# A Trainium2 kernel's start-up rebuilt: two plain first steps, a first chunk in halves, later operand sums, halo rows from DRAM

## The chip, the cores and the metric

The kernel runs on one core of one Trainium2 chip. The metric is the device time of one execution in microseconds; the time before is 1448.68 us, the median of three runs (1447.93 to 1449.42).

## The reference

Two layers follow each other. The first is a causal convolution of seven taps along the sequence, with softmax weights per head of 24 channels. The second turns each value into a phase pair, mixes the tokens with two 4224 x 4224 matrices and ends with a channel mix.

```python
# x: (8, 4224, 192), weight: (8, 7); w = softmax(weight) over the taps
x_pad = concat([zeros((B, 6, D)), x], axis=1)
x = einsum('hk,bskhg->bshg', w, unfold(x_pad, 7))      # the convolution

theta = x @ w_theta                                    # (192, 192)
zr, zi = x * cos(theta), x * sin(theta)
yr = einsum('ts,bsd->btd', w_tok_r, zr)                # (4224, 4224)
yi = einsum('ts,bsd->btd', w_tok_i, zi)
u = x + yr + yi
out = u + maximum(u @ w_ch, 0)
```

All inputs and the output are float32; the kernel computes in float16 with float32 sums.

## The kernel before

**Tiles.** The 4224 tokens are cut into 33 chunks of 128 on the input side (`NK`) and 33 blocks of 128 on the output side (`NT`). A chunk is not 128 neighbouring tokens: it takes 32 (`Q`) from each quarter of the sequence (`token`). All 8 batches and 192 channels lie side by side, 1536 columns, and these are split into two halves of each batch's channels, 768 columns each (`HN`).

**A chunk's life** (class `Chunk`, line 177). `__init__` loads x into `xw`, casting to float16, with four DMAs from Pool (line 197), one for each quarter, and gives every 32 tokens 16 rows of history in front (`HALO`), so `xw` has 2 x 48 rows. The history of most chunks is copied from the chunk before, inside the chip's memory, by four DMAs on SP (line 188); chunks 0, 11 and 22 read it from DRAM with their own rows. `conv(j)` is called twice, for four heads each: eight products with a banded matrix (line 210, tile `pc`), one copy out of PSUM by ACT (line 151) or DVE (line 149), and after the second call four stores of the convolved x to DRAM scratch `xs` (SP, line 227). `transpose` turns x through TensorE (line 165, tile `tp`) and copies it to `uT`. `theta(g)` multiplies half of the batches with w_theta (line 141, tile `v`), and ACT takes cosine and sine of it (line 246). `product` multiplies x with these (line 251), which gives four operands: Z11 and Z12 are cosine times x for the two channel halves, Z21 and Z22 sine times x. `sums` makes from them the combined operands T1 to T4 (line 257, four subtractions).

**Seven products for eight.** A step works on a pair of output blocks. Mixing two blocks, two matrices and two channel halves would take eight products of a weight tile with an operand for each chunk. A scheme in the manner of Winograd and Strassen does it with seven (`runs`, line 409): it needs the combined operands T1 to T4 and four combined weights S1 to S4 (`wsum`, line 348). A "cell" below is one such product for one chunk: two TensorE instructions of 384 columns on line 443. Cells go run by run, and within a run chunk by chunk. A run's sum in PSUM tile `y` (two buffers) is given to the block's sum `pv` by `give`: by an ACT copy (line 406) where it is the first to come there in the first wave, by a DVE add (line 408) otherwise. In a paired step of the first wave these are four copies and three adds.

**Steps.** Seventeen units (16 pairs and one single block) are visited in 58 steps. Chunks enter in three waves of 11 (`NW`). In the first wave few chunks exist yet, so step 0 has 2 chunks, step 1 has 4, then 5, 7, 9 and 11. The weights of a step come as two loads `st` (m = 1 for w_tok_r, 2 for w_tok_i; four DMAs each from Pool, line 323; two buffers); `turn` transposes a 32 x 32 block pattern out of `st` into `wt` on DVE (line 336, nine buffers). "11" and "21" are the first and second block's tiles of the first matrix, "12" and "22" of the second. So a load of step t + 2 can only start when the two turns of step t + 1 from that buffer are done.

**The order of the work.** TensorE, DVE, ACT and some Pool instructions are chained in the order in which the program emits them (`pe`, `dve`, `act`, `pool`, lines 84 to 94). The x loads and the SP copies are not chained and are queued as the framework places them. Each step carries a list of events (`w_tasks`, `step_events`): a function and a place, in sevenths of the step; `mix` emits it when the step's cells have come that far. Outputs are placed by the steps' planned times (`self.time`, 0.324 us for a cell).

**The build loop** (lines 662 to 709) starts everything. Round i convolves chunk i, makes the phases and products of chunk i - 1, loads chunk i + 3, and between these puts up to 11 cells of the stream by calls of `between`, if their chunk is ready (`ready`); in rounds 1 and 2 slots that stay empty get filler products on zeros (`idle`, line 588), which do nothing but keep TensorE running. `conv`, `theta` and `transpose` share two PSUM buffers.

Of the kernel before, what the change touches and what calls it, by code (L numbers as in the profile page):

```python
# [16 lines left out]
def kernel(  # L17
# [23 lines left out]
    nc = tc.nc  # L41
# [11 lines left out]
    NT = S // P  # L53
    HALO = 16
    WR = Q + HALO
# [5 lines left out]
    NW = 11  # L61
    PC = 512

    base = [0, 0, 1, 1, 2, 3, 3, 4, 4, 5, 5]
# [109 lines left out]

    Z11, T1, Z21, Z22, T2, T4, T3 = range(7)

    class Chunk:


        def __init__(self, k, before=None):  # L180
            self.k = k
            self.xw = wk.tile([2 * WR, 2, B, D], F16, name="xw", tag="big", bufs=6)
            for a in range(NQ):
                h, lo = a // 2, (a % 2) * WR
                t0 = token(k, a)
                hist = self.xw[lo : lo + HALO, h, :, :]
                if before is not None:
                    nc.sync.dma_start(
                        out=hist, in_=before.xw[lo + Q : lo + Q + HALO, h, :, :]
                    )  # L190
                elif t0 == 0:
                    nc.vector.memset(hist, 0.0)
                else:
                    lo, t0 = lo - HALO, t0 - HALO
                lo += HALO
                n = (a % 2 + 1) * WR - lo
                nc.gpsimd.dma_start(  # L197
                    out=self.xw[lo : lo + n, h, :, :],
                    in_=x[:, t0 : t0 + n, :].rearrange("b s d -> s b d"),
                )  # L200

        def conv(self, j):
# [5 lines left out]
            for h in range(4):  # L208
# [12 lines left out]
                pc[:, :, 0 : 2 * B * G].rearrange("p i (h b g) -> p i h b g", h=2, b=B),  # L221
                self.k == 0 and j == 1,
            )
            if j == 1:
                for a in range(NQ):
                    t0 = token(self.k, a)
                    nc.sync.dma_start(
                        out=xs[t0 : t0 + Q, :], in_=self.x[a * Q : (a + 1) * Q, :]
                    )

        def transpose(self):
            self.xT = turned()
            transposed(self.xT, self.x, range(NG), self.k < 2)

        def theta(self, g):
# [3 lines left out]
            for first, bias in ((Z11, half_pi[:]), (Z21, None)):  # L239
                o = self.z[:, first : first + 2, :].rearrange(  # L240
                    "p h (k b e) -> p k b h e", b=2, e=HD
                )[:, 2 * g : 2 * g + 2, :, :, :]
                args = dict(out=o, in_=v, func=AT.Sin)
                if bias is not None:
                    args.update(bias=bias, scale=1.0)
                act(nc.scalar.activation(**args))  # L246

        def product(self, first):
            o = self.z[:, first : first + 2, :].rearrange("p h (b e) -> p h b e", e=HD)
            xv = self.x.rearrange("p (b h e) -> p h b e", h=2, e=HD)  # L250
            dve(nc.vector.tensor_tensor(out=o, in0=xv, in1=o, op=ALU.mult))  # L251

        def sums(self, which):
            z = self.z
            for o, a, b in (((T3, Z22, T1), (T1, T1, Z11)),
                            ((T2, Z22, T1), (T4, Z21, T2)))[which]:
                dve(nc.vector.tensor_tensor(  # L257
                    out=z[:, o, :], in0=z[:, a, :], in1=z[:, b, :], op=ALU.subtract
                ))

# [14 lines left out]
    def load_chunk(k):  # L275
        if k < NK and k not in chunks:
            chunks[k] = Chunk(k, before=chunks[k - 1] if k % NW else None)

# [6 lines left out]
    class Step:  # L285


        def __init__(self, t):
# [10 lines left out]
            for i, tb in enumerate(self.tbs):  # L299
# [5 lines left out]
                else:  # L305
                    far = known <= start[2 * NW - 1]
                    self.ahead.append((i, 2 * NU - NW + 2 * (t % NU) if far else start[-1],
                                       (t // NU - 1 - far) % 2))
            self.time = 0.324 * self.n * (7 if self.pair else 4)
            self.st, self.w, self.xr, self.ub, self.uT, self.pv = {}, {}, {}, {}, {}, []  # L310
# [43 lines left out]
        def w_tasks(self):  # L354

            if not self.pair:
                return [(0.25, lambda: self.turn("11")), (4.2, lambda: self.turn("12"))]
            return [
                (0.25, lambda: self.turn("11")), (1.2, lambda: self.turn("21")),
# [50 lines left out]
        def runs(self):  # L410
# [17 lines left out]
            ]  # L428

        def mix(self, events):  # L430

            runs = self.runs()
            events = sorted(events, key=lambda e: e[0])
            y = {}
            for r, (wn, zn, cn, opens, to) in enumerate(runs):
                if opens:
                    y[cn] = ypool.tile([P, 2, PC], F32, name="y", tag="y")
                for c, k in enumerate(self.ks):
                    while events and events[0][0] * len(runs) <= 7 * (r + c / self.n):
                        events.pop(0)[1]()  # L440
                    yield k
                    for q in range(2):
                        pe(nc.tensor.matmul(  # L443
                            y[cn][:, q, 0:BH],
                            lhsT=self.w[wn][:, c, :, :].rearrange("p bt i -> p (bt i)"),
                            rhs=chunks[k].z[:, zn, q * BH : (q + 1) * BH],
                            start=(opens and c == 0), stop=(c == self.n - 1),
                            skip_group_check=True,
                        ))
                if to:  # L450
# [55 lines left out]

    steps = [Step(t) for t in range(NSTEP)]
    outputs = [
        (sum(s.time for s in steps[: t + 1]) + at, f)
# [3 lines left out]
    def step_events(t):  # L513
# [11 lines left out]
        if t + 2 < NSTEP:  # L525
            nxt = steps[t + 2]
            for m in (1, 2):
                found.append((1.3 + 3 * (m - 1), lambda m=m: nxt.load_w(m)))
        if t == NU - 2:
            def load_wch():  # L530
# [129 lines left out]
    for m in (1, 2):  # L660
        steps[1].load_w(m)
    for i in range(NW + 2):
        ch = chunks.get(i) if i < NW else None
        old = chunks[i - 1] if 0 < i <= NW else None

        def between(n):
            left = more(n)
            if 0 < i < 3:
                idle(min(left, 2))

# [3 lines left out]
        if old:  # L674
            old.theta(0)
        between(1)
        if ch:
            ch.conv(1)
        if i == 0:
            idle(4)  # L680
        ready[0] = i - 2
        between(2)
        if old:
            old.theta(1)
        if i == 1:
            for at, f in steps[0].w_tasks():
                if at < 2.2:
                    f()
        if i + 3 < NW:
            load_chunk(i + 3)  # L690
        between(1)
        if ch:
            ch.transpose()
        if old:
            old.product(Z11)
        between(2)
        if i == 1:
            for at, f in steps[0].w_tasks():
                if at >= 2.2:
                    f()  # L700
        if old:
            old.product(Z21)
        between(1)
        if old:
            old.sums(0)
        between(1)
        if old:
            old.sums(1)
# [35 lines left out]
```

## Time and profile before

| what | value |
|---|---|
| median of three runs | 1448.68 us |
| span of the profiled execution, first to last instruction | 1444.6 us |
| TensorE products on line 443 | 7656 of 128x384, 1283.6 us busy |
| mean granted TensorE clock | 0.997 |
| chain that ended last, TensorE's share | 89% |
| first convolution product | 8.89 us |
| x loads in the first 70 us | 44, line 197 |

A span is shorter than the time of a run, since a run also has what lies before the first and after the last instruction. In a timeline row the first two numbers are start and length of a group in us, then come engine, line, operation and operands, and in brackets how long the engine idled before and who released it. Products on TensorE overlap, so a group's length contains the last one's tail.

### The profile page before, as it was taken

The page shows a single profiled execution, that of the slowest core. Times are in us where ns is not written, and L with a number is a line of the kernel's source. Part 1 is how long each engine was busy: PE and PEld are TensorE (multiplying, and loading weights), DVE is VectorE, ACT ScalarE, POOL GpSimd, SP SyncE. Part 2 cuts the span into 40 slices and gives each one's busy share as a digit, 9 for nine tenths or more (in the row PEclk, how much of TensorE's full clock was granted, in tenths as well). Part 3 has the DMA queues.
Part 4 walks back from the last instruction along what each step waited for, and adds up shares of the span by engine and source line. Part 5 has one row for each costly group of instructions (what it writes and reads, how often), then busy time and mean ns, then how long its engine had stood idle before and what let it go on. Part 6 is the DMA issues. An engine that isn't in the chain of part 4 may idle for free.

```text
span 1444.6 us, 23749 instructions
## 1 busy us (share of the span) xinstructions
PE 1414.5 (98%) x9809; PEld 886.3 (61%) x9809; DVE 978.2 (68%) x1050; ACT 316.2 (22%) x379; POOL 434.6 (30%) x655
## 2 busy tenths in 40 slices
PE   7899999999999999999999999999999999999997
PEld 4656666666666666666666666666666666666665
DVE  6893554555448687866666657876877677767686
ACT  6851101111124254000000004435210110010133
POOL 8421211111223232432433343233323123213120
PEclk9999999999999999999999999999999999999999
DMA  9975756564699999897899889989999999898883
GB/s 181 253 148 136 146 119 133 98 152 87 152 229 210 226 244 222 219 265 173 223 245 222 233 155 239 235 181 237 274 220 202 213 204 221 204 200 193 166 232 116
DMA packets 272029, 281.99 MB, mean 195 GB/s; under 512 B 106672, under 2 KB 240176, under 8 KB 271920
## 3 DMA queue, kind: packets, MB, share of 16 engines
q0 software_dynamic: 162464, 92.15, 48.4%
q1 hardware_dynamic: 71824, 178.88, 35.2%
q10 hardware_dynamic: 37632, 9.44, 4.3%
q8 instruction: 77, 1.26, 0.4%
q14 instruction: 32, 0.26, 0.1%
HBM read 245.49 MB, written 108.13 MB: 245 GB/s over the span
## 4 chain that ended last, share of the span: by engine, by line
PE 89%; DVE 3%; DMA 2%; ACT 2%; POOL 1%; issue 1%; SPq 0%; DVEq 0%; ACTq 0%; POOLq 0%
PE y L443 81%; PE v L141 5%; PE pc L210 1%; PE tp L165 1%; ACT z L246 1%; DVE pv L408 1%; DMA xw<-xw 1%; POOL xw L197 1%; DMA xw<-in_x_dram 1%; DVE z L257 1%; POOL st L323 1%; DVE z L251 1%; DMA pv<-part 1%; ACT uT L151 1%; DVE wt L336 0%
## 5 line engine op out<-in xcount | busy, mean ns | idle before, releaser
L443 PE MATMUL y<-z,wt 128*128 128x384 f16 x7656 | 1283.6, 326 | 10.4 <-DVE pv L408 7.3
L443 PEld LDWEIGHTS <-wt 128*128 128x128 f16 x7656 | 740.7, 98 | 488.1 <-issue 10.2
L408 DVE TENSOR_TENSOR pv<-y,pv 128x768 f32<-128x768 f32 x324 | 309.2, 955 | 327.0 <-PE y L443 286.8
L336 DVE STREAM_TRANSPOSE wt<-st 128x1408 f16<-128x1408 f16 (+7 forms) x224 | 327.8, 1465 | 45.8 <-PE y L443 39.1
L323 POOL DMA_DIRECT2D st<-in_moe_w_tok_r_dram x232 | 132.4, 579 | 464.9 <-DVE wt L336 459.4
L323 POOL DMA_DIRECT2D st<-in_moe_w_tok_i_dram x232 | 132.5, 580 | 405.4 <-DVE wt L336 397.5
L348 DVE TENSOR_TENSOR wt<-wt 128x1408 f16<-128x1408 f16 (+7 forms) x216 | 176.1, 815 | 40.5 <-PE y L443 38.0
L151 ACT ACTIVATE z<-pc 128x768 f16<-128x768 f32 x65 | 53.3, 820 | 386.7 <-PE pc L210 386.5
L151 ACT ACTIVATE ub<-pv 128x768 f16<-128x768 f32 x63 | 50.2, 835 | 333.2 <-DVE pv L408 310.7
L406 ACT ACTIVATE pv<-y 128x768 f32<-128x768 f32 x66 | 54.0, 819 | 281.6 <-PE y L443 281.6
L141 PEld LDWEIGHTS <-uT 128*128 128x128 f16 x1056 | 91.1, 98 | 27.4 <-issue 8.5
L386 POOL TENSOR_TENSOR pv<-pv,xr 128x1536 f32<-128x1536 f32 x24 | 74.5, 3105 | 67.1 <-DVE pv L476 21.9
L197 POOL DMA_DIRECT2D xw<-in_x_dram x132 | 76.5, 591 | 30.1 <-DMA xw<-xw 9.7
L476 DVE SCALAR_TENSOR_TENSOR pv<-v,pv 128x768 f32<-128x768 f32 x66 | 62.9, 954 | 27.5 <-PE v L141 27.0
L151 ACT ACTIVATE uT<-tp 128x1536 f16<-128x1536 f16 (+1 forms) x49 | 59.7, 1221 | 74.4 <-PE tp L165 74.4
L257 DVE TENSOR_TENSOR z<-z 128x768 f16<-128x768 f16 x132 | 73.4, 556 | 3.6
L246 ACT ACTIVATE z<-v,half_pi 128x768 f16<-128x768 f32 x66 | 59.9, 907 | 42.1 <-PE v L141 41.7
L251 DVE TENSOR_TENSOR z<-z 128x1536 f16<-128x1536 f16 x66 | 60.1, 948 | 6.6 <-ACT z L246 6.6
L141 PE MATMUL v<-wth,uT 128*128 128x192 f16 x528 | 55.0, 248 | 5.6 <-ACT z L246 3.3
L141 PE MATMUL v<-wch,uT 128*128 128x192 f16 x528 | 54.2, 246 | 2.1 <-DVE pv L476 1.2
L246 ACT ACTIVATE z<-v 128x768 f16<-128x768 f32 x66 | 53.5, 810 | 0.0
L210 PE MATMUL pc<-xw,bands 96*64 96x192 f16 x528 | 35.3, 256 | 1.2 <-DVE bands L628 0.8
(43 smaller groups left out, 138.0 us busy)
## 6 DMA issues: line engine op xcount, KB each, us to landing
part<-pv SPq DMA_DIRECT2D x79, 768.0 KB, 4.6
pv<-part SPq DMA_DIRECT2D x79, 768.0 KB, 6.0
out_dram<-pv SPq DMA_DIRECT2D x66, 384.0 KB, 4.3
st<-in_moe_w_tok_r_dram POOLq DMA_DIRECT2D x136, 176.0 KB, 5.7
st<-in_moe_w_tok_i_dram POOLq DMA_DIRECT2D x136, 176.0 KB, 5.1
xs<-z SPq DMA_DIRECT2D x132, 96.0 KB, 4.1
xw<-in_x_dram POOLq DMA_DIRECT2D x121, 96.0 KB, 5.9
xr<-xs SPq DMA_DIRECT2D x24, 384.0 KB, 4.5
```

The source lines that it names most:

```text
L141: pe(nc.tensor.matmul(v[:, k, b * D : (b + 1) * D], lhsT=tT[:, 3 * k + b + i, :], rhs=w[:, 2 * b + i, :], start=(i == 0), stop=(i == 1),))
L151: act(nc.scalar.activation(out=out, in_=in_, func=AT.Copy))
L197: nc.gpsimd.dma_start(out=self.xw[lo : lo + n, h, :, :], in_=x[:, t0 : t0 + n, :].rearrange("b s d -> s b d"),)
L246: act(nc.scalar.activation(**args))
L251: dve(nc.vector.tensor_tensor(out=o, in0=xv, in1=o, op=ALU.mult))
L257: dve(nc.vector.tensor_tensor(out=z[:, o, :], in0=z[:, a, :], in1=z[:, b, :], op=ALU.subtract))
L323: pool(nc.gpsimd.dma_start(out=st[a * Q : (a + 1) * Q, 0:nb, :, 0:n] .rearrange("i r bt s -> i (r bt) s"), in_=w[self.tbs[0] * P : (self.t ...
L336: dve(nc.vector.transpose(self.w[name][:, 0 : self.n, :, :], self.st[int(name[1])][:, int(name[0]) - 1, :, 0 : self.n * Q] .rearrange("p b ...
L348: dve(nc.vector.tensor_tensor(out=self.w[name][:, 0 : self.n, :, :], in0=self.w[a][:, 0 : self.n, :, :], in1=self.w[b][:, 0 : self.n, :, : ...
L386: ins = pool(nc.gpsimd.tensor_tensor(out=self.pv[i], in0=self.pv[i], in1=self.xr[i], op=ALU.add))
L408: dve(nc.vector.tensor_tensor(out=o, in0=yv, in1=o, op=ALU.add))
L443: pe(nc.tensor.matmul(y[cn][:, q, 0:BH], lhsT=self.w[wn][:, c, :, :].rearrange("p bt i -> p (bt i)"), rhs=chunks[k].z[:, zn, q * BH : (q + ...
```

## The change

There are four parts.

1. Steps 0 and 1 (`plain`: first wave, a pair, at most `NP` = 4 chunks) compute eight plain products from Z11, Z12, Z21 and Z22, with no S and no T. The first block's four products go chunk by chunk, the second block's run by run. All four gives of a step are copies. The turns of their weights stand at other places of the step before.
2. Chunk 0 is convolved by batch halves (`conv_batches`, `transpose_batches`): sixteen products of 96 columns for each half, the copies shared by ACT and DVE. Which engine copies what changes for chunks 1 to 3 as well. Chunk 0's products are made by batch halves too. There are 12 fillers fewer.
3. Chunks 0 to 3 get their sums T1, T2 and T4 during step 1 and T3 during step 2 instead of in their build round. Z12 takes the place of T3 in memory.
4. `HALO` is 6. Every load reads its history from DRAM with its own rows, so it has 38 rows (32 for the very first), and there are no copies from chunk to chunk.

```diff
-    HALO = 16
+    HALO = KS - 1
+    NP = 4
...
+    Z12 = T3
...
             for a in range(NQ):
                 h, lo = a // 2, (a % 2) * WR
-                t0 = token(k, a)
-                hist = self.xw[lo : lo + HALO, h, :, :]
-                if before is not None:
-                    nc.sync.dma_start(
-                        out=hist, in_=before.xw[lo + Q : lo + Q + HALO, h, :, :]
-                    )
-                elif t0 == 0:
-                    nc.vector.memset(hist, 0.0)
-                else:
-                    lo, t0 = lo - HALO, t0 - HALO
-                lo += HALO
-                n = (a % 2 + 1) * WR - lo
+                t0 = token(k, a) - HALO
+                n = WR
+                if t0 < 0:
+                    nc.vector.memset(self.xw[0:HALO, 0, :, :], 0.0)
+                    lo, t0, n = HALO, 0, Q
                 nc.gpsimd.dma_start(
...
-                self.k == 0 and j == 1,
+                self.k == 1 or (self.k in (2, 3) and j == 1),
...
+        def conv_batches(self, g):
...
+            pc = banks("pc")
+            for h in range(H):
+                for half in range(2):
+                    pe(nc.tensor.matmul(
+                        pc[half * 2 * Q : (half + 1) * 2 * Q, h // 4,
+                           h % 4 * GB * G : (h % 4 + 1) * GB * G],
+                        lhsT=bands[:, h, :, :].rearrange("p a m -> p (a m)"),
+                        rhs=self.xw[:, half, g * GB : (g + 1) * GB, h * G : (h + 1) * G],
+                        start=True, stop=True,
+                    ))
+            for i in range(2):
+                evacuate(
...
+                    i == 1,
+                )
...
         def transpose(self):
             self.xT = turned()
-            transposed(self.xT, self.x, range(NG), self.k < 2)
+            transposed(self.xT, self.x, range(NG), self.k < 4)
+
+        def transpose_batches(self, g):
+            if g == 0:
+                self.xT = turned()
+            transposed(self.xT, self.x, [g], True)
...
         def sums(self, which):
+            for o, a, b in (((T1, Z12, Z11), (T3, Z22, Z12)),
+                            ((T2, Z22, T1), (T4, Z21, T2)))[which]:
+                self.sum(o, a, b)
...
-            self.time = 0.324 * self.n * (7 if self.pair else 4)
+            self.plain = self.first and self.pair and self.n <= NP
+            self.time = 0.324 * self.n * (8 if self.plain else 7 if self.pair else 4)
...
+            if self.plain:
+                return [
+                    (3.6, lambda: self.turn("11")), (4.2, lambda: self.turn("21")),
+                    (5.0, lambda: self.turn("12")), (6.0, lambda: self.turn("22")),
+                ]
...
+            for i, name in enumerate(("c1", "c2")):
+                a, b = f"{i + 1}1", f"{i + 1}2"
+                cells = [
+                    (r, c, h) + w for c in range(self.n) for h in range(2)
+                    for r, w in enumerate(((a, (Z11, Z12)[h]), (b, (Z21, Z22)[h])))
+                ]
+                if i:
+                    cells.sort(key=lambda e: (e[2], e[0]))
+                for r, c, h, wn, zn in cells:
+                    done = r == 1 and c == self.n - 1
+                    yield (wn, zn, f"c{h + 1}", c, r == 0 and c == 0, done,
+                           (i, h, True) if done else None)
...
+        if t in (NPS, NPS + 1):
+            for j, k in enumerate(k for k in range(NK) if start[k] <= NPS):
+                for o, a, b, at in (
+                    ((T1, Z12, Z11, 0), (T2, Z22, T1, 0.3), (T4, Z21, T2, 0.6)),
+                    ((T3, Z22, Z12, 0),),
+                )[t - NPS]:
+                    found.append((
+                        (1.3 + 1.4 * j if t == NPS else 1.2 + 0.6 * j) + at,
+                        lambda k=k, o=o, a=a, b=b: chunks[k].sum(o, a, b),
+                    ))
...
-    for i in range(NW + 2):
+    for g in range(NG):
+        chunks[0].conv_batches(g)
+    idle(2)
+    for g in range(NG):
+        chunks[0].transpose_batches(g)
+    for i in range(1, NW + 2):
...
-            if 0 < i < 3:
-                idle(min(left, 2))
+            if i < 3:
+                idle(min(left, 2) if i == 1 else 0)
...
         if i == 1:
-            for at, f in steps[0].w_tasks():
-                if at < 2.2:
-                    f()
+            for name in ("11", "21"):
+                steps[0].turn(name)
         if i + 3 < NW:
             load_chunk(i + 3)
         between(1)
+        if i == 1:
+            for first in (Z11, Z21):
+                old.product(first, slice(0, 1))
         if ch:
             ch.transpose()
-        if old:
+        if i == 1:
+            for first in (Z11, Z21):
+                old.product(first, slice(1, 2))
+        elif old:
             old.product(Z11)
         between(2)
         if i == 1:
-            for at, f in steps[0].w_tasks():
-                if at >= 2.2:
-                    f()
-        if old:
+            for name in ("12", "22"):
+                steps[0].turn(name)
+        elif old:
             old.product(Z21)
         between(1)
-        if old:
+        if old and start[i - 1] > NPS:
             old.sums(0)
```

The operands keep their meaning: T1 is now written beside Z12 instead of over it, since Z12 is needed by the plain products, and T3 is made last, over Z12. `NPS` is the last plain step, 1. In `mix` the cells come from a list (`products`), and an event's place counts sevenths of that list.

## The prediction

> **What bounds the kernel now.** I read the page first.
>
> ```profile
> span 1444.6 us, 23749 instructions
> PE 1414.5 (98%) x9809; PEld 886.3 (61%) x9809; DVE 978.2 (68%) x1050; ACT 316.2 (22%) x379; POOL 434.6 (30%) x655
> PE   7899999999999999999999999999999999999997
> ```
>
> From the fourth slice on TensorE is full, so the kernel is as long as TensorE's work plus the time TensorE loses, and that is lost in the first 105 us. There the timeline of TensorE shows 12.6 us of waits after the first convolution (8.89), the last being 2.31 us at 102.48, and 25 filler products of 0.163 us, 4.1 us: 16.7 us is all that this change can win. So I cut the start into stretches of 20 us (columns: time busy of PE, PEld, DVE, ACT, POOL; granted clock; DMA share; GB/s).
>
> ```profile
> 20.00:40.00 20.00, 15.10 (x138) 9.74 (x136) 18.78 (x33) 15.76 (x20) 13.24 (x24) 0.91 1.31 211
> 40.00:60.00 20.00, 17.71 (x176) 12.16 (x175) 14.95 (x23) 19.00 (x24) 11.02 (x21) 1.00 1.29 248
> 60.00:80.00 20.00, 18.41 (x177) 12.41 (x175) 18.07 (x27) 18.70 (x24) 5.61 (x10) 1.00 1.06 230
> 80.00:100.00 20.00, 19.11 (x151) 12.43 (x148) 19.53 (x27) 13.09 (x16) 4.55 (x8) 1.00 0.81 177
> ```
>
> DVE is the full engine from 20 to 40, ACT from 40 to 80, DVE again from 80 to 100. How DVE stops TensorE stands in the timeline of PE.
>
> ```profile
> 32.25 0.81 PE L443 MATMUL y<-z,wt 128*128 128x384 f16 x4 [1.13 <-ACT pv L406]
> 34.29 0.48 PE L443 MATMUL y<-z,wt 128*128 128x384 f16 x2 [1.23 <-ACT pv L406]
> ...
> 36.44 0.82 PE L443 MATMUL y<-z,wt 128*128 128x384 f16 x2 [0.78 <-DVE pv L408]
> 37.05 1.49 PE L141 MATMUL v<-wth,uT 128*128 128x192 f16 x8
> ...
> 43.12 0.59 PE L210 MATMUL pc<-xw,bands 96*64 96x192 f16 x8 [0.22 <-ACT z L246]
> ```
>
> Products of step 0 wait for y banks to be emptied, the phase products of chunk 3 (37.05) queue behind them, and ACT idles 2.49 us for those. Round 4 of the build loop takes from 34.71 to 43.12, 8.4 us, where later ones take 7.1 to 8.0. The clock falls as well (the 13th number):
>
> ```profile
> 36.00:38.00 2.00, 1.56 (x8) 1.19 (x9) 1.97 (x5) 0.08 (x1) 0.00 (x0) 0.54 1.27 242
> 38.00:40.00 2.00, 2.00 (x16) 1.12 (x14) 2.00 (x4) 1.43 (x2) 1.65 (x3) 0.60 1.35 254
> ```
>
> Last the timeline of Pool, which issues x and the token weights in one queue.
>
> ```profile
> 21.56 2.28 POOL L323 DMA_DIRECT2D st<-in_moe_w_tok_i_dram  x4 [1.38 <-DVE wt L336]
> 23.83 4.55 POOL L197 DMA_DIRECT2D xw<-in_x_dram  x8
> 30.45 2.42 POOL L323 DMA_DIRECT2D st<-in_moe_w_tok_r_dram  x4 [2.07 <-DVE wt L336]
> 32.87 2.30 POOL L197 DMA_DIRECT2D xw<-in_x_dram  x4
> ```
>
> The x8 are chunks 4 and 5; the load at 30.45 is step 2's first, which waits until DVE has turned "21" of step 1 out of the buffer; chunk 6 stands behind it although its own buffer is long free.
>
> **Plain products.** Steps 0 and 1 get one run more: 2 + 4 cells of 0.324 us (two products at 0.162: the 54 from 91.23 take 8.94 us, 0.17 of it the last one's tail), +1.95 us on TensorE. DVE loses eight weight sums (4 x 0.29 and 4 x 0.42 by their rows: 2.8 us) and six adds into pv (0.95 each: 5.7 us); ACT keeps its four copies a step. The cells now go chunk by chunk: step 0 has four that need only chunk 0, so round 2 runs 4 cells where it ran 1, and round 5 runs 11 where it ran 8. Counting slots round by round, the loop ends with 10 cells more done; less the 6 added, 4 x 0.324 = 1.3 us of work has moved into the loop.
>
> **Operand sums later.** Sixteen subtractions (0.555 alone, 0.53 in a row, 8.5 us) leave DVE's full stretch and come back in steps 1 and 2.
>
> **Copies moved to DVE.** Chunk 1's two convolution copies, one each of chunks 2 and 3 (0.96 by DVE for 0.7 by ACT in a row), less chunk 0's, which becomes two halves, and the transposed copies of chunks 2 and 3 (0.96 by DVE for 1.45 by ACT). About 5 us go onto DVE, less than the sums and adds taken away, and as much off ACT.
>
> **Chunk 0 in halves.** 32 products of 96 columns replace 16 of 192. The trace has no 96-column product: between half of 0.065 each (no cost) and the same 0.065 (+1.0 us); I take a middle, 0.85 us a half. The half copies (384 wide) lie between 0.41 and 0.81; I take 0.5. The halves overlap: convolution to 10.6, copies to 11.2, transposes to 12.0, copy to 12.7, so the phase products start at 12.75, not 13.80.
>
> **Following that down.** Chunk 1's phase products need the sines of chunk 0 off the two shared PSUM buffers, as before (13.7 + 4 x 0.8 with the product of 0.8 between), and its transposed copy ends at 17.8, not 19.04. Chunk 2's sits on DVE: its phase products start at 23.6, not 26.13. Chunk 3's at 28.7, not 37.05, since DVE has no sums and no adds there. The 12 fillers dropped stood in waits, so they cost nothing while the clock holds; round 2 has 3.1 us of real work in 3.4 by my count, so I let it hold.
>
> **The halo.** Forty SP copies of 48 KB in the start vanish, and the wait of each for its neighbour; the chain of waits gives them 4.4%, but the one at 55.91 to 64.78 lies under ACT's full stretch, so I count nothing. Pool still issues 44 loads, of 38 rows in place of 32 or 48, which take 0.58 and about 0.65. Their landing:
>
> ```profile
> L197 POOL DMA_DIRECT2D xw<-in_x_dram x44: 576/583/730, 1.4 to 62.8; - x44
> ...
> DMA to landing us min/median/max: 3.0/4.7/10.2
> ```
>
> No row shows 38 rows. In the first 5 us 32 rows land in 4.2 us and 48 rows in 4.6, so the near bound is 4.2 to 4.6 and the far one 10.2, the slowest of the tile. I take 4.6, nearest in size. [...]
>
> **The new wait.** Step 0's plan turns "11" and "21" of step 1 at 3.6 and 4.2 sevenths (it was 0.25 and 1.2), while step 2's first load is still asked for at 1.3. In emission order that load now stands in round 2, ahead of chunk 5's; it cannot start before "21" has left the buffer, and that follows chunk 3's transposed copy on DVE (28.65), one product (0.9) and two transposes (0.63 each): 30.85. Queued behind it on Pool are chunk 5, chunk 6 and step 2's second load. So: weights 30.95 to 33.25, chunk 5 issued to 35.55, last part from 34.98, landed 39.6. Without the wait its convolution would run at 35.5; it runs at 39.6, against 43.12 before: -3.5 us. DVE waits too: "11" of step 2 needs the load landed (36.4), with chunk 3's operand products (two of 0.92) behind it: done 39, before 44.2, so it is no later than chunk 5.
> TensorE idles some 3.5 us before 39.6, about what preceded the half clock above (1.5 us of work in 3.4). I charge one more such 3.4 us spell: 1.7 us of work lost, of which a round has about 0.7 to spare: +1.0.
>
> **From round 5 on.** ACT does the same: two copies, four sines, one transposed copy, 5.9 us, and the give copies. DVE gets 6.4 us net of the late sums (chunk 3's fell here before too) less step 1's three adds, 2.85: +3.6 us, into about 5.9 us that it idles between 47 and 98. I take nothing; without that cover it is up to 3.6.
>
> **Sum.** -3.5 (round 5) -1.3 (cells in the loop; the 1.95 is inside) +1.0 (clock) = -3.8. Against the profiled execution: 1444.6 - 3.8 = 1440.8; the median 1448.68 is 4.1 above that span, which I keep: 1444.9.
>
> **Rivals.** *Late loads* (slower). If loads of 38 rows take the slowest landing, 10.2, chunk 0's last part (issued 3.38) lands at 13.6: the start slips 4.7, "21" with it, chunk 5 is issued to 40.2 and lands at 49.8, +6.7 against 43.12; less 1.3, 1454.1. It decides above about 7.5 us of landing; below that start and chunk 5 together cost less than the gain. For it: the width is new and DMA share is over 1.2 until 60 us. Against: 32 and 48 rows differ by 0.4.
> *DVE takes over.* The 3.6 us find no room, because DVE's gaps are waits for TensorE (1.43 at 80.06) that stay: -3.8 + 3.6, 1448.5. For it: DVE is already full from 80 to 100.
> *Pool's order is another.* If chunk 5 is put ahead of the blocked weights, round 5 starts at 35.5: -7.6 -1.3, no clock loss, but +2 for DVE's wait on those weights: -6.9, 1441.8. For it: on SP stores of chunk 0 (11.45) went ahead of halo copies emitted earlier. Against: Pool kept emission order through waits of 1.38 and 2.07 us.
>
> **How the numbers follow.** Forecast 0.40, Pool's order 0.20, DVE 0.18, late loads 0.22. A measurement of this kernel tells about 0.2%, 2.9 us, from no change: faster is below 1445.8, slower above 1451.6. Faster: 0.20 and most of the forecast, 0.57 with what leans over from it; same 0.21; slower 0.22. The range takes in Pool's order and its spread below, 1440, and part of late loads above, 1452.5; the forecast's own is 1442.5 to 1447.
>
> **What would show it.** First phase products near 12.75; those of chunk 3 near 28.7; a Pool wait of about 6 us before step 2's first weights, with chunk 5's loads behind, and its convolution near 39.6 after an idle TensorE, the clock low just then; DVE over 95% busy from 45 to 90. Wrong if xw lands later than 7 us, if chunk 5's loads come before those weights, or if the first saturated stretch starts no earlier than 102.

## The result, and the profile after

The changed kernel takes 1592.4 us (median of five, 1585.05 to 1593.36) where the kernel before takes 1448.4 (five, 1447.65 to 1449.42): the ratio is 1.0977, 95% interval 1.096 to 1.0995. The forecast of 1444.9 has the wrong sign, and the time lies 140 us above the top of its range.

The page of the changed kernel first: span, busy times, TensorE and its granted clock by slices, Pool's DMA queue, two groups of instructions (busy and mean ns, then idle before and its releaser), and the row of the x loads (KB, us to landing).

```profile
span 1583.3 us, 23454 instructions
PE 1452.4 (92%) x9825; PEld 904.7 (57%) x9825; DVE 972.6 (61%) x1046; ACT 312.6 (20%) x374; POOL 547.9 (35%) x655
PE   4568999999998796999999999698799999999997
...
PEclk6788999999999898999999999899899999999999
...
q0 software_dynamic: 446112, 95.14, 61.4%
...
L192 POOL DMA_DIRECT2D xw<-in_x_dram x132 | 189.2, 1438 | 131.2 <-DMA xw<-in_x_dram 54.3
...
L205 PE MATMUL pc<-xw,bands 76*64 76x192 f16 x512 | 45.4, 289 | 95.0 <-DMA xw<-in_x_dram 94.3
...
xw<-in_x_dram POOLq DMA_DIRECT2D x131, 114.0 KB, 13.3
```

The row of TensorE has holes in three places: the start, slices 13 to 16 and slices 26 to 29, which are the three waves in which chunks are built. The x loads now take Pool 1438 ns each to issue and land 13.3 us after the issue began (median). Pool's queue carries 446,112 packets. The same rows of the page before have 591 ns, 5.9 us, 1.2 us of idle TensorE ahead of the convolution in place of 95.0, and little over a third of the packets in nearly the same bytes:

```profile
q0 software_dynamic: 162464, 92.15, 48.4%
...
L197 POOL DMA_DIRECT2D xw<-in_x_dram x132 | 76.5, 591 | 30.1 <-DMA xw<-xw 9.7
...
L210 PE MATMUL pc<-xw,bands 96*64 96x192 f16 x528 | 35.3, 256 | 1.2 <-DVE bands L628 0.8
...
xw<-in_x_dram POOLq DMA_DIRECT2D x121, 96.0 KB, 5.9
```

The chain of waits of the changed kernel from 497 us on (start, length, what) shows what holds the second wave; before, the chain from 500 to 540 us is TensorE without a break.

```profile
496.78 15.64 DMA xw<-in_x_dram
512.42 0.28 issue
512.70 20.10 DMA xw<-in_x_dram
532.81 0.04 issue
532.85 0.84 PE pc L205 x7
```

The timeline of TensorE, changed kernel (start, length, group, in brackets the idle time before and its releaser):

```profile
15.00 1.49 PE L230 MATMUL pc<-xw,bands 76*64 76x96 f16 x31 [3.43 <-DMA xw<-in_x_dram]
...
24.94 0.85 PE L205 MATMUL pc<-xw,bands 76*64 76x192 f16 x7 [4.61 <-DMA xw<-in_x_dram]
...
162.51 17.72 PE L509 MATMUL y<-z,wt 128*128 128x384 f16 x108 [1.83 <-DVE pv L452]
...
521.73 0.27 PE L205 MATMUL pc<-xw,bands 76*64 76x192 f16 x1
532.85 0.84 PE L205 MATMUL pc<-xw,bands 76*64 76x192 f16 x7 [10.85 <-DMA xw<-in_x_dram]
```

At 521.73 one product of the convolution runs, and the other seven wait 10.85 us for a later load of the same tile. The first long stretch without a wait begins at 162.51, against 102.48 before: 60.0 of the 138.7 us by which the span grew. For the two later waves, the windows of the changed kernel (length, busy PE, PEld, DVE, ACT, POOL, clock, DMA share, GB/s):

```profile
400.00:500.00 100.00, 95.32 (x628) 57.84 (x627) 45.07 (x43) 19.73 (x23) 37.04 (x46) 1.00 0.93 160
500.00:600.00 100.00, 87.64 (x643) 55.48 (x642) 67.86 (x84) 32.86 (x38) 43.68 (x45) 0.91 1.24 177
600.00:700.00 100.00, 85.60 (x601) 53.04 (x599) 64.25 (x74) 26.22 (x30) 37.67 (x43) 0.91 1.11 200
...
900.00:1000.00 100.00, 94.81 (x632) 57.87 (x630) 65.62 (x70) 12.32 (x14) 51.16 (x49) 0.99 1.06 178
1000.00:1100.00 100.00, 88.35 (x648) 54.92 (x649) 62.69 (x76) 32.65 (x37) 44.26 (x46) 0.94 1.26 172
1100.00:1200.00 100.00, 86.96 (x590) 53.76 (x588) 61.88 (x69) 26.29 (x30) 33.90 (x43) 0.93 1.07 211
```

TensorE is idle for 31.4 us of the first three windows and 29.9 of the last three (before: 0.7 and 2.1 in the same windows). That is 58.4 us more, and the clock falls to 0.91 with the waits. 60.0 and 58.4 leave some 20 of the 138.7, which fits work done at the lower clock; that last share is argued, not shown.

Why the loads are late can be counted. A token row of a load is 8 runs of 384 bytes, one for each batch (the trace has 42,512 packets of 384 bytes against 37,632 before, 4,880 more for 610 more rows), so 38 rows are 304 data packets. Sorted by size, Pool's queue holds this (counts of the packets in each trace):

```
kernel               packets   of 4 bytes   extra 4-byte packets for each of 131 loads
before (32, 48 rows)  162464         9888
48 rows               177824         9888        0
39 rows               177824        19320       72
40 rows               194592        35040      192
38 rows (after)       446112       288656     2128
```

The trace doesn't name the engine of a packet, so how many engines share a load is my estimate from these counts. 2128 is 14 x 152, and 152 is half of 304: as if each of two engines had 152 data packets, 19 of the 38 rows, and each of the fourteen others, of the 16 that the page counts, as many packets of 4 bytes. Reckoned in the same way, 39 rows come to 13 engines with 3 rows, 24 packets, each (3 x 24 = 72), 40 rows to 10 with 4 rows, 32 packets, each (6 x 32 = 192), and the loads of 48 rows, with no extra packets, to all 16. No other number of engines gives these counts by that reckoning.

The starts of the packets agree with the estimate of two engines. From 24.5 to 25.3 us of the changed kernel the 384-byte packets begin in two series, one at 24.509, 24.541, 24.572 and so on, the other at 24.531, 24.563, 24.595: a packet lasts 51 ns, and the next of its series begins 32 ns after it. By that step, 152 in a row take an estimated 4.8 us and 24 take 0.8. The difference, 4.1 us, and the longer issue (0.8 us, as landing is counted from the issue's start) make 4.9 of the 7.3 us between the median landing with 39 rows (6.0) and with 38 (13.3), and about the whole step between the shortest landings of each (4.3 and 8.7). The rest of the median's step isn't accounted for.

Pool pays twice. Each issue is 2.4 times as long, and then it waits, as the waits of the changed kernel show (engine, line, what for; us in all, times, longest):

```profile
PE pc L205 <- DMA xw<-in_x_dram: 94.3, 26, 11.1
...
DVE wt L375 <- DMA st<-in_moe_w_tok_i_dram: 63.0, 10, 13.9
POOL xw L192 <- DMA xw<-in_x_dram: 54.3, 32, 5.0
...
POOL st L362 <- DMA xw<-in_x_dram: 39.2, 25, 4.8
```

and as its timeline shows it from inside:

```profile
7.81 6.38 POOL L192 DMA_DIRECT2D xw<-in_x_dram  x4
14.18 2.31 POOL L362 DMA_DIRECT2D st<-in_moe_w_tok_r_dram  x4
17.92 1.44 POOL L192 DMA_DIRECT2D xw<-in_x_dram  x1 [1.44 <-DMA xw<-in_x_dram]
20.16 1.44 POOL L192 DMA_DIRECT2D xw<-in_x_dram  x1 [0.80 <-DMA xw<-in_x_dram]
22.60 1.43 POOL L192 DMA_DIRECT2D xw<-in_x_dram  x1 [1.00 <-DMA xw<-in_x_dram]
```

After its first twelve issues Pool waits ahead of each x load shown here. The semaphores in the trace say for what: Pool's 618 DMAs take eight semaphores in turn, and an issue waits until the DMA that used its semaphore last, the eighth before it, has landed. So at most eight are under way (none of the 610 issues of this trace that have an eighth before them begins before that one has landed), and x loads that land late hold back the issues behind them: 65 such waits, 104.3 us in all, where the kernel before has 10, 10.8 us. The token weights stand in the same queue, and DVE waits 63.0 us for those of `w_tok_i` (4.1 before).

### The profile page after: what moved, and what is told of

Its sections match the earlier page's. It is cut to its first block, busy times and chain, and to the rows that moved or that the text cites. A ratio compares the mean times of both kernels' runs of the same rounds, so it can differ in the third digit from the quotient of the medians.

```text
span 1583.3 us, 23454 instructions
## 1 busy us (share of the span) xinstructions
PE 1452.4 (92%) x9825; PEld 904.7 (57%) x9825; DVE 972.6 (61%) x1046; ACT 312.6 (20%) x374; POOL 547.9 (35%) x655
## 3 DMA queue, kind: packets, MB, share of 16 engines
q0 software_dynamic: 446112, 95.14, 61.4%
q10 hardware_dynamic: 37632, 9.44, 3.7%
## 4 chain that ended last, share of the span: by engine, by line
PE 70%; DMA 21%; POOL 3%; DVE 3%; issue 2%; ACT 1%; DVEq 0%; POOLq 0%; ACTq 0%
PE y L509 66%; DMA xw<-in_x_dram 17%; DMA st<-in_moe_w_tok_i_dram 4%; PE v L142 4%; POOL xw L192 3%; PE pc L205 1%; DVE pv L452 1%; PE tp L166 1%; DMA part<-pv 1%; DVE pv L542 0%; DVE z L286 0%; DVE wt L387 0%; DVE z L295 0%; DVE wt L375 0%; POOL st L362 0%
## 5 line engine op out<-in xcount | busy, mean ns | idle before, releaser
L509 PE MATMUL y<-z,wt 128*128 128x384 f16 x7668 | 1304.6, 329 | 16.1 <-DVE pv L452 15.1
L192 POOL DMA_DIRECT2D xw<-in_x_dram x132 | 189.2, 1438 | 131.2 <-DMA xw<-in_x_dram 54.3
L387 DVE TENSOR_TENSOR wt<-wt 128x1408 f16<-128x1408 f16 (+6 forms) x208 | 172.6, 830 | 40.2 <-PE y L509 38.4
L152 ACT ACTIVATE z<-pc 128x768 f16<-128x768 f32 (+1 forms) x62 | 49.6, 801 | 487.2 <-PE pc L205 477.5
L205 PE MATMUL pc<-xw,bands 76*64 76x192 f16 x512 | 45.4, 289 | 95.0 <-DMA xw<-in_x_dram 94.3
L152 ACT ACTIVATE ub<-pv 128x768 f16<-128x768 f32 x63 | 50.2, 835 | 337.4 <-DVE pv L452 307.8
L142 PEld LDWEIGHTS <-uT 128*128 128x128 f16 x1056 | 97.8, 103 | 25.8 <-issue 8.3
L205 PEld LDWEIGHTS <-bands 76*64 76x64 f16 x512 | 25.9, 124 | 121.5 <-DMA xw<-in_x_dram 79.8
L286 DVE TENSOR_TENSOR z<-z 128x1536 f16<-128x1536 f16 (+1 forms) x68 | 60.7, 927 | 10.4 <-ACT z L280 10.3
L142 PE MATMUL v<-wth,uT 128*128 128x192 f16 x528 | 63.3, 271 | 1.2 <-ACT uT L152 0.6
## 6 DMA issues: line engine op xcount, KB each, us to landing
xw<-in_x_dram POOLq DMA_DIRECT2D x131, 114.0 KB, 13.3
```

Of the source, the lines that this page charges most:

```text
L142: pe(nc.tensor.matmul(v[:, k, b * D : (b + 1) * D], lhsT=tT[:, 3 * k + b + i, :], rhs=w[:, 2 * b + i, :], start=(i == 0), stop=(i == 1),))
L152: act(nc.scalar.activation(out=out, in_=in_, func=AT.Copy))
L192: nc.gpsimd.dma_start(out=self.xw[lo : lo + n, h, :, :], in_=x[:, t0 : t0 + n, :].rearrange("b s d -> s b d"),)
L205: pe(nc.tensor.matmul(pc[half * 2 * Q : (half + 1) * 2 * Q, h // 2, h % 2 * B * G : (h % 2 + 1) * B * G], lhsT=bands[:, 4 * j + h, :, :].r ...
L387: dve(nc.vector.tensor_tensor(out=self.w[name][:, 0 : self.n, :, :], in0=self.w[a][:, 0 : self.n, :, :], in1=self.w[b][:, 0 : self.n, :, : ...
L509: pe(nc.tensor.matmul(y[cn][:, q, 0:BH], lhsT=self.w[wn][:, c, :, :].rearrange("p bt i -> p (bt i)"), rhs=chunks[k].z[:, zn, q * BH : (q + ...
```

## The experiments

Theory A was that the 38 rows themselves cost the time, through the few engines that the estimate above gives such a load. B was that reading the halo from DRAM does, whatever the width. C was that the other parts do (the plain products, the halves, the moved sums).

**48 rows from DRAM.**

```
-    HALO = KS - 1
+    HALO = 16
```


> The changed kernel with 16 history rows in place of 6, still read from DRAM with the chunk's own rows, so loads have 48 rows. [...] Expected: 24 row pieces for each engine, no extra packets, Pool issue near 0.65 us, landing near 5 us, time 1439 to 1447, as the other three parts were forecast at 1444.9. Theory B (history from DRAM, whatever the width: more bytes, rows read twice): 48 rows read 26% more than 38, so it stays near 1590 or gets worse. Theory C (the plain steps, the late sums and Pool's order cost the time): stays above 1500.

1448.19 us, ratio 1.0003 (0.9994 to 1.0012). All of the loss is gone, with more bytes loaded. The time is a little above the expected 1439 to 1447, and the landing, 6.5 us at the median, above the expected 5.

**39 rows.**

```
-    HALO = KS - 1
+    HALO = 7
```


> The changed kernel with 7 history rows, so loads have 39 rows, one more than 38. Theory A: 39 is divided by 13, so 13 engines with 24 row pieces each; extra packets of 4 bytes 3 x 24 = 72 for each load; landing near 5 us; time within 3 us of the 48-row run. Theory B: one row more cannot help, near 1590. A theory in which any width that is no multiple of 16 falls into the slow case gives near 1590 too.

1448.35 us, 0.9995 (0.9983 to 1.0006). One more row, and the page of this kernel reads:

```profile
span 1446.6 us, 23454 instructions
...
q0 software_dynamic: 177824, 94.46, 50.4%
...
L192 POOL DMA_DIRECT2D xw<-in_x_dram x132 | 87.5, 672 | 49.0 <-DMA st<-in_moe_w_tok_r_dram 17.3
...
xw<-in_x_dram POOLq DMA_DIRECT2D x131, 117.0 KB, 6.0
```

Only the number of rows differs from the changed kernel, by one; the packets fall by 2048 for each of the 131 loads, which is 16 x (152 - 24) by the estimate above, the issue falls to 672 ns and the landing to 6.0 us. B and C fall as causes of the loss.

**40 rows.**

```
-    HALO = KS - 1
+    HALO = 8
```


> The changed kernel with 8 history rows, so loads have 40 rows. Theory A: 8 engines with 40 row pieces each, 8 x 40 = 320 extra packets of 4 bytes; landing in between, near 6 us (13.3 us for 152 pieces and about 4.7 for 24 give 0.067 us a piece: 5.8); Pool issue about 0.75 us; time 0 to 8 us above the 39-row run. A rule of multiples of 16 or of powers of two puts it with 38 or with 48 instead.

1449.4 us, 1.0007 (0.9998 to 1.0016). The expected number of extra packets, 320 for 8 engines, was wrong: 192 were found, which is 10 engines by the estimate above.

**The kernel before with 38 rows alone.** Only the constructor of the changed `Chunk` and its `HALO = KS - 1` are put into the kernel before.

```
-    HALO = 16
+    HALO = KS - 1
...
-        def __init__(self, k, before=None):
+        def __init__(self, k):
...
+                t0 = token(k, a) - HALO
+                n = WR
```


> The kernel before with the history of the change only: 38-row loads from DRAM, no copies from chunk to chunk; steps, sums and build loop as before. Theory A: all of the loss comes from here, 1575 to 1605. Theory C: near 1448, within 5 us.

1594.32 us, 1.1003 (1.0978 to 1.1027): this part alone brings the whole loss. The page:

```profile
span 1593.6 us, 23450 instructions
...
q0 software_dynamic: 446112, 95.14, 60.9%
...
xw<-in_x_dram POOLq DMA_DIRECT2D x131, 114.0 KB, 12.8
```

**38 rows as 6 and 32.** The changed kernel, each load issued as two.

```
+                cuts = [(0, n)] if n == Q else [(0, HALO), (HALO, n)]
+                for c0, c1 in cuts:
+                    nc.gpsimd.dma_start(
+                        out=self.xw[lo + c0 : lo + c1, h, :, :],
+                        in_=x[:, t0 + c0 : t0 + c1, :].rearrange("b s d -> s b d"),
```


> The changed kernel itself, 6 history rows from DRAM, the same bytes from the same addresses into the same places, but each 38-row load issued as two, 6 rows and 32 rows. Theory A: 6 rows go to 6 engines in 8 pieces each (80 extra packets of 4 bytes), 32 rows to 16 engines; no 152-piece loads. Twice the issues on Pool, about 1.0 us for a pair against 1.44. Time 1447 to 1455, that is 135 us or more back. If the rows' addresses or the short history in itself were the cause, it stays near 1590.

1476.01 us, 1.0195 (1.0181 to 1.0209). The packets are gone, and 116 of the 144 us with them, but not all: the expected 1447 to 1455 was missed. From the page:

```profile
q0 software_dynamic: 179920, 94.07, 49.5%
...
L194 POOL DMA_DIRECT2D xw<-in_x_dram x263 | 150.7, 587 | 75.7 <-DMA st<-in_moe_w_tok_r_dram 38.1
...
L207 PE MATMUL pc<-xw,bands 76*64 76x192 f16 x512 | 38.0, 261 | 26.3 <-DMA xw<-in_x_dram 23.9
```

The pieces land after 4.4 and 4.6 us, sooner than any other form, yet TensorE still waits 23.9 us for x. A load of 6 rows takes Pool 0.58 us like one of 32, so 263 of them take 150.7 us of a queue that has the weights in it too, and twice as many loads go through the same eight semaphores (38 waits for the eighth DMA before, 50.2 us; with 39 rows 13, 26.3 us). The expectation had left these out. That they are what is left of the loss is argued; no run takes one of them away.

**The other parts alone.** The changed kernel with the 16-row copies and loads of before.

```
-        def __init__(self, k):
+        def __init__(self, k, before=None):
...
-            chunks[k] = Chunk(k)
+            chunks[k] = Chunk(k, before=chunks[k - 1] if k % NW else None)
```


> The changed kernel with the history as the kernel before had it (16 rows, copied from chunk to chunk on SP, loads of 32 rows): parts 1 to 3 of the change alone. Theory H (history from DRAM costs a little at any width, because a load has 24 pieces for each engine in place of 16 while the DMA engines are full until 60 us): faster than the 39-row run, 1443 to 1446. If the width beyond the engine count does not matter, the same as the 39-row run, 1447 to 1449.

1449.78 us, 1.0007 (0.9998 to 1.0015): the forecast's gain of 3.8 isn't there without the 38 rows either, and the expectation that a load of 32 rows beats one of 39 failed. Part of the reason may be in two lines of Pool's timeline in the kernel with 39 rows:

```profile
32.56 2.31 POOL L362 DMA_DIRECT2D st<-in_moe_w_tok_r_dram  x4 [5.81 <-DVE wt L375]
34.86 5.24 POOL L192 DMA_DIRECT2D xw<-in_x_dram  x8
```

The wait that the prediction named is there, 5.81 us, with chunks 5 and 6 behind it; 7.18 us with the copies. The next three kernels shorten it.

**Chunk 5 first, then earlier turns, on 39 rows.** First the load event of step 2 in step 0 goes from 1.3 to 1.8; then the turns of a plain step are moved as well.

```
-                found.append((1.3 + 3 * (m - 1), lambda m=m: nxt.load_w(m)))
+                found.append(((1.8 if t == 0 and m == 1 else 1.3 + 3 * (m - 1)),
+                              lambda m=m: nxt.load_w(m)))
...
-                    (3.6, lambda: self.turn("11")), (4.2, lambda: self.turn("21")),
-                    (5.0, lambda: self.turn("12")), (6.0, lambda: self.turn("22")),
+                    (1.9, lambda: self.turn("11")), (2.3, lambda: self.turn("21")),
+                    (4.2, lambda: self.turn("12")), (5.0, lambda: self.turn("22")),
```


> 39-row loads, and step 2's first weight load asked for at 1.8 sevenths of step 0 in place of 1.3, so that chunk 5's load stands ahead of it on Pool. In the 39-row run this weight load waited 5.81 us on Pool for the turn of step 1, chunk 5's loads came at 34.86, and its convolution ended its wait for them at 45.30 where the kernel before ran it at 43.12. Theory P (the new wait on Pool has eaten the gain of the other parts): chunk 5 is issued near 27 us, its convolution runs near 38 to 40, time 1442 to 1446. Theory D (the gain is lost to DVE later, to the late sums): no change, 1447 to 1449.

> As the run before, and the turns of step 1 at 1.9, 2.3, 4.2 and 5.0 sevenths of step 0 in place of 3.6, 4.2, 5.0 and 6.0, so the two weight buffers come free earlier and DVE's 3.59 and 6.88 us waits for step 2's weights shrink. Theory P: the weight load of step 2 starts near 29 in place of 32.6, another 1 to 3 us, time 1440 to 1444. Theory D: 1447 to 1449.

1446.93 us, 0.9989 (0.9981 to 0.9998), and 1446.8, 0.9987 (0.9977 to 0.9997). The intervals overlap that of the plain 39 rows; a small gain at most. Both missed the ranges expected if this wait had eaten the gain (1442 to 1446 and 1440 to 1444), though the first did what it was meant to: chunk 5's convolution runs at 39.04 in place of 45.30. TensorE then gains 3.5 us from 40 to 60 (busy 17.57 us for 14.04) and loses 3.7 from 60 to 80 (15.61 for 19.27), where DVE is busy 19.73 of 20 and TensorE waits 3.49 us for it at 79.41: what the move wins is lost again at DVE.

**Both moves with the copies.** The same diff, on the kernel with the copies of before.

> Parts 1 to 3 with the copies, and both moves of the run with 39 rows (chunk 5 first, earlier turns of step 1). Theories P and H together: the fastest, 1438 to 1443. Theory D: 1447 to 1449.

1443.88 us, 0.9966 (0.9955 to 0.9977), against 1.0007 without the moves: here they are worth some 6 us. Pool's timeline of this kernel has the eight loads of chunks 4 and 5 first, and the wait is 1.08:

```profile
24.13 4.56 POOL L199 DMA_DIRECT2D xw<-in_x_dram  x8
29.77 2.42 POOL L369 DMA_DIRECT2D st<-in_moe_w_tok_r_dram  x4 [1.08 <-DVE wt L382]
```

**Three of the four operand sums back in the build loop.** T1, T2 and T4 of chunks 0 to 3, made in their own rounds as before; T3 stays late, for it overwrites Z12. Once with the copies, once with 39 rows, both with the two moves.

```
-                    ((T1, Z12, Z11, 0), (T2, Z22, T1, 0.3), (T4, Z21, T2, 0.6)),
+                    (),
...
+        elif old:
+            old.sum(T1, Z12, Z11)
         between(1)
-        if old and start[i - 1] > NPS:
+        if old:
             old.sums(1)
```


> The fastest kernel so far (copies, chunk 5 first, earlier turns; 0.9966 of before) with T1, T2 and T4 of chunks 0 to 3 made in their build round again, T3 alone left late since it lies over Z12. In that fastest kernel DVE was busy 12.34 of 20 us from 20 to 40 and 19.76 from 60 to 80, without a gap from 46.6 to 84. Theory D2 (the late sums fill DVE and hold the build loop up after 60 us): 12 subtractions of 0.53 us, 6.4 us, go back into the idle stretch; DVE below 19 of 20 from 60 to 80 and 1 to 4 us faster, 1440 to 1443. Rival (ACT holds the loop, DVE's full stretch costs nothing): 1443 to 1445, or slower where the sums delay the early rounds.

> The 39-row kernel with chunk 5 first and earlier turns (0.9987 of before), T1, T2 and T4 of chunks 0 to 3 in their build round again. Theory D2: 1442 to 1445, most of its 4.04 us wait for DVE at 80.80 gone. Rival: no change, 1446 to 1448.

With the copies nothing moves: 1443.61 us, 0.9972 (0.9961 to 0.9982). With 39 rows it is 1441.33 us (1440.42 to 1442.54), 0.9957 (0.9945 to 0.997), clearly under the 0.9987 without it, and the fastest kernel here. The windows of 20 us, first with late sums, then with early ones:

```profile
20.00:40.00 20.00, 17.34 (x174) 11.76 (x172) 10.98 (x16) 16.01 (x21) 14.93 (x25) 1.00 1.37 206
60.00:80.00 20.00, 14.76 (x137) 9.60 (x135) 19.73 (x33) 15.79 (x20) 8.95 (x15) 1.00 1.15 196
```

```profile
20.00:40.00 20.00, 17.35 (x165) 11.06 (x162) 15.34 (x24) 15.70 (x21) 16.31 (x27) 1.00 1.42 213
60.00:80.00 20.00, 18.32 (x174) 11.82 (x171) 19.79 (x30) 17.50 (x22) 8.79 (x15) 1.00 1.21 210
```

DVE, the third busy time, had 9 us free from 20 to 40 and is full from 60 to 80. Sums moved from the second stretch into the first cost TensorE nothing there (17.34 and 17.35) and give it 3.6 us later. The wait that goes stands in the timeline of TensorE with the late sums:

```profile
80.80 0.80 PE L509 MATMUL y<-z,wt 128*128 128x384 f16 x2 [4.04 <-DVE pv L452]
```

With the copies TensorE gains from 60 to 80 too (18.50 for 16.73), but loses as much from 40 to 60 (16.24 for 18.45). There its timeline has a new wait of chunk 5's convolution, for an SP copy of history, 43.62 where it was 41.22 without the move:

```profile
43.62 0.49 PE L212 MATMUL pc<-xw,bands 96*64 96x192 f16 x7 [2.70 <-DMA xw<-xw]
```

Why that copy comes later was not followed up.

**The kernel before with 39 rows alone.** As in the kernel before with 38 rows, but `HALO = 7`.

> The kernel before with nothing but the history of the 39-row run (7 rows from DRAM, no copies; steps, sums and build loop as before). It says to whom the 0.43% of the fastest run (39 rows, chunk 5 first, earlier turns and early T sums) belongs. If the mended parts 1 to 3 bring it: within 2 us of before, 1446 to 1450. If dropping the SP copies brings it: 1441 to 1444.

1445.32 us, 0.9981 (0.997 to 0.9992): the halo from DRAM, dropping the copies, is itself a small gain once the width is a good one. It lies between the two outcomes expected. Parts 1 to 3 as they stand add nothing to it (0.9995 with them, 0.9981 without, the intervals overlapping); only with both moves and the early sums do they come out ahead (0.9957).

## Why the prediction was wrong

One table carries most of it: where TensorE's first long stretch without a wait starts (its timeline), the span, and the difference.

```
kernel                          stretch from   span     rest
before                             102.48    1444.6   1342.1
48 rows                            107.03    1448.0   1341.0
39 rows                            105.45    1446.6   1341.2
copies, other parts alone          106.48    1448.1   1341.6
copies, both moves                 100.25    1441.5   1341.3
39 rows, both moves                104.80    1445.9   1341.1
39 rows, both moves, early sums     97.49    1438.7   1341.2
before, 39 rows                    101.52    1443.2   1341.7
6 and 32 rows                      110.49    1472.2   1361.7
after                              162.51    1583.3   1420.8
```

Where the loads are good, the rest is 1341 to 1342 us whatever is changed, so the prediction was right to price the change by its start there. With 38 rows 79 us are lost behind the start as well.

**The step that failed** is the landing of the 38-row loads: "I take 4.6, nearest in size". The runs have 13.3 us to landing and 1.44 us of Pool's time to issue, where "about 0.65" was taken. Nearness in rows was the wrong measure: 39 rows land in 6.0 us, near the 5.9 of 32 and the 6.5 of 48, and 38 rows in 13.3. What goes with that is the number of extra packets, 2128 a load against 72 and none, from which the estimate above has two engines against 13 and 16. The number of engines, which the expectations count with, no run shows directly; the runs showed these counts and times in its place. The far bound, 10.2, was too low as well, and was a single late transfer of an unchanged size. The prediction said that no row showed 38, and then let the nearest row decide.

**The slower rival, late loads**, had the right mechanism, but 1454.1 as its price. It moved the start by one late tile and counted chunk 5 once. It left out that every load pays, so Pool falls further behind each time, that Pool waits for its own landings (54.3 us ahead of x loads, 39.2 ahead of weights), that the weights queue there too, and that the second and third waves, which were taken as hidden, wait for the same loads.

**The forecast's own steps**, read where the loads are good (39 rows): the first phase products are at 13.82 (forecast 12.75, before 13.80), since the transposes took 1.49 us and a convolution of 0.85 went ahead; the halves of chunk 0 bring nothing. Chunk 2's are at 24.85 (23.6; before 26.13), so half of that gain is real. Chunk 3's are at 33.36 (28.7; before 37.05).

The Pool wait was right in place and kind, 5.81 us for about 6. What followed was dearer than the forecast, as TensorE's timeline with 39 rows shows:

```profile
41.41 0.24 PE L205 MATMUL pc<-xw,bands 78*64 78x192 f16 x1 [1.67 <-DMA xw<-in_x_dram]
45.30 0.85 PE L205 MATMUL pc<-xw,bands 78*64 78x192 f16 x7 [3.65 <-DMA xw<-in_x_dram]
```

Chunk 5 is complete at 45.30 and not 39.6, later than the 43.12 of before: the term of -3.5 becomes a loss. Taking the delay away wasn't enough: chunk 5 first brought its convolution to 39.04, but the time fell by 1.4 us only, for the rest was lost again in DVE's full stretch from 60 to 80. Step 2's second weights, behind the same queue, hold DVE for another 6.88 us until 50.13. The clock of the window from 40 to 60 is 0.83, which is 0.17 x 20 / 0.5 = 6.8 us at half clock where one spell of 3.4 was charged (from 46 to 50 the clock reads 0.50). The sign that DVE would be over 95% busy from 45 to 90 didn't come: it is 36.87 of 45 us with 39 rows, mostly because it waits for these weights.

**DVE's late sums** were taken as nothing, up to 3.6 without cover. With 39 rows and the moves the cover wasn't there: taking three of four away from DVE's full stretch brought 1446.8 down to 1441.3; with the copies the same move gave nothing. So the rival in which DVE takes over had a real mechanism with 39 rows, hidden here under a far larger loss.

**Pool's order** wasn't another: the blocked weights stayed ahead of chunk 5, as the forecast had it. Put the other way by hand, with the earlier turns, it gave 1443.88 with the copies, near the 1441.8 that the rival worked out, but chunk 5's convolution came at 40.74 and not at 35.5, so the nearness is in part luck; with 39 rows it gave 1446.8.

## What to carry to other kernels

When an edit changes how many rows a Pool load has, don't take its cost from the nearest number, and count the packets of its queue: here 38 rows made 446,112 packets and cost 10% of this kernel, 39 made 177,824 and cost nothing. Price a slower load for every place that issues it, its engine's own time included, not only at the first wait for it, and look how many DMAs that engine has under way: here, on eight semaphores, the ninth waits for the first. And before an early load is left waiting for a buffer, look at what stands behind it in the same queue: here, asking for it later, together with earlier turns, was worth 6 us with the copies and little with 39 rows.

## What the runs showed of the hardware

- The 618 Pool DMAs of the kernel before have 9,888 packets of 4 bytes, 16 for each. A load of 38 rows has 2128 more, one of 39 rows 72, one of 40 rows 192, a piece of 6 rows 80 (179,920 packets in the kernel with 6 and 32 rows), one of 48 rows none. By my estimate from these counts, each engine without a share of a load gets as many of them as an engine with a share has data packets. One lasts 9 ns at the median in the changed kernel, but all of Pool's together last 4,082 us there (211 before), against 2,409 for its packets of 384 bytes. The issue on Pool grew from 0.58 us (32 rows) over 0.67 (39) and 0.72 (40) to 1.44 (38), which by the estimate are 16, 24, 32 and 152 data packets on each engine with a share.
- In each of the two series of the changed kernel's trace from 24.5 to 25.3 us the packets of 384 bytes last 51 ns and begin every 32, so one isn't finished before the next begins. If a series is one engine's, as the counts suggest, that engine overlaps its packets.
- From 24.5 to 25.3 us 62 packets of 384 bytes begin in a microsecond there, from 32.0 to 33.5 us 125: twice as many, by the estimate two pairs of engines at once. The trace doesn't name the engine of a packet, so which pair a load gets stays open.
- In these traces Pool had at most eight DMAs under way: by the semaphores each waits for the landing of the eighth before it. How much that costs depends on the landing: 104.3 us of waits with 38 rows, 26.3 with 39, 10.8 in the kernel before.
- In the split loads a piece of 6 rows (18 KB) took Pool 0.58 us to issue, like one of 32 rows (96 KB).
